# A 32-byte constant at the bottom of SBUF: moving every left-hand tile by half of 64 bytes

## The chip, the cores and the metric

The kernel runs on one core of one Trainium2 chip. The metric is the device time of one execution in microseconds (us); the time before is the median of 3 runs. The profile is that of one execution, with its own time beside it.

## What is computed

Band attention with 32 global tokens per sequence, followed by two MLPs of the same size, all in float32.

```python
# attention: 4 sequences x 8 heads, 32 global + 512 local tokens, head size 64
s_g = scale * q_g @ k_all.T;  out_g = softmax(s_g) @ v_all         # global rows see everything
s_l = [q_l @ k_g.T, band(q_l @ k_l.T, 32)] * scale                 # local rows: globals and a band
x = concat([out_g, softmax(s_l) @ [v_g, v_l]])                     # 2176 tokens x 512
# first MLP: ELU; second MLP: a smooth ReLU
x = elu(x @ w_in) @ w_out                 # 512 -> 2048 -> 512
h = x @ w2_in
g = where(h >= 1, h, where(h <= -1, 0, (h + 1)**2 / 4))
out = g @ w2_out
```

## The kernel before

The time after attention is matrix multiplication. Every float32 operand is split into a high and a low part (`xh`/`xl` for tokens, `gh`/`gl` for activations, `wh`/`wl` for weights), and each product is three matmuls: low weights with high tokens, high with low, high with high.

**Products.** `Up.products` (lines 258 and 261) multiplies tokens with w_in, `down` (line 342) and `down_rows` (line 359) multiply activations with w_out. In lines 261 and 342 the weights (128 columns) are the stationary operand, and 512 columns of `xh`/`xl` or `gh`/`gl` are the moving one. The 128 global tokens (index `GR`, tiles `xh4`, `xl4`) are handled the other way round in lines 258 and 359: a token or activation tile is stationary, and the weights move past it, 128 columns for each block of the hidden layer in line 258, 512 at once in line 359.

**Stages.** The 16 blocks of 128 hidden units of each layer are taken in ten chunks, `CHUNKS = [(3, 4, 3, 4, 2), (4, 3, 4, 3, 2)]`. The weights of a chunk lie in one of two rings, taken in turn: chunks 0, 2, 4, 6, 8 use ring 0 (`wh0`, `wl0`, three blocks deep), chunks 1, 3, 5, 7, 9 use ring 1 (`wh1`, `wl1`, four deep).

```python
n = max(len(fs) for _, fs in chunks[i::2])
ring[i] = [pool.tile([P, n, WCOLS], F32R, name=f"w{nm}{i}") for nm in "hl"]
```

While one ring is multiplied, `prep` fills the other: DMA of the raw float64 words, then ScalarE and VectorE. The `up` products of one chunk overlap the last `down` products of the one before (`LAG`), so there are short stretches in which both rings are used. In the profiled execution ring 1 is alone in use at about 192 to 264, 355 to 431, 498 to 574, 664 to 746 and 835 to 875 us, and ring 0 at 284 to 339, 593 to 647 and 765 to 819 us. Chunk 0 runs inside the attention.

**Where the numbers of matmuls come from.** A chunk of n blocks has 4 sequences x n blocks x 12 matmuls in line 261 and as many in line 342, and for the global tokens 12 in line 258 (n x 128 columns wide) and 3n in line 359 (512 wide).

**Between the products.** ScalarE and VectorE apply the curve and split the activations. A finished bank goes through `collect`: ScalarE copies it into one of two `ev` tiles (line 317), which a DMA writes or, on GpSimd's queue, adds to DRAM (lines 319 and 321). The last chunk of a layer loads these sums (`sum`, line 340), adds them (line 323), and splits them (lines 326 and 327) or writes the output (line 329).

**Order.** In the attention every instruction stays in program order (`Pinned`); behind it a planner orders them.

**Places in SBUF.** Pools take their room from the bottom in the order of opening, or from the top with `side="right"`. A tile begins at a multiple of 32 bytes, so a [128, 1] tile of 4 bytes takes 32. Places below are bytes from the start of a partition, and what is left of them modulo 64:

| tiles | side | place | modulo 64 |
|---|---|---|---|
| `mask_sb`, `eye_sb`, `half_sb` | left | 16512, 18048, 18560 | 0 |
| `one_sb`, the last constant | left | 18592 | 32 |
| `xh0` to `xl4` | left | 18624 to 88256 | 0 |
| `g`, `gh`, `gl` | left | 88256 to 112832 | 0 |
| ring 0: `wh0`, `wl0` | left | 112832, 125120 | 0 |
| `ev`, `acc_rows` | left | 137408 to 143552 | 0 |
| ring 1: `wh1`, `wl1` | right | 163808, 180192 | 32 |
| `wraw`, `top`, `power`, `rest`, `sum` (behind the attention) | right | 196576 and up | 32 |

All offsets inside these tiles that a matmul uses are multiples of 512 bytes, so an operand's place modulo 64 is that of its tile.

Of the kernel before, what the change touches and what calls it, by code (L numbers as in the profile page):

```python
# [9 lines left out]
F32 = mybir.dt.float32  # L10
# [15 lines left out]
P = 128  # L26
# [42 lines left out]
def band_attention_then_two_mlps(  # L69
# [20 lines left out]
    const = ctx.enter_context(tc.tile_pool(name="const", bufs=1))  # L90
# [7 lines left out]
    eye_sb = const.tile([P, P], F32, name="eye_sb")  # L98
    half_sb = const.tile([P, 1], F32, name="half_sb")
    one_sb = const.tile([P, 1], F32, name="one_sb")  # L100
    sizes = [SL] * B + [B * SG]
    xh = [xpool.tile([P, KT, n], F32R, name=f"xh{j}") for j, n in enumerate(sizes)]
    xl = [xpool.tile([P, KT, n], F32R, name=f"xl{j}") for j, n in enumerate(sizes)]
# [25 lines left out]
    eng = pinned  # L129
# [269 lines left out]
    with ExitStack() as actx:  # L399
# [46 lines left out]
        def spread_keys(b, hp):  # L446

            k_sb = loaded[b, hp][1]
            right = k_sb[:, KPAD:].rearrange("p (a c) -> p a c", a=NSUB)
            after = k_sb[:, SG + 32:KPAD].rearrange("p (a c) -> p a c", a=NSUB)  # L450
            glob = k_sb[:, 0:SG].rearrange("p (o c) -> p o c", o=1)

            if b + hp == 0:
                eng.vector.tensor_copy(right[:, :, 0:32], after)
                eng.scalar.activation(
                    right[:, :, 32:64], glob.to_broadcast([P, NSUB, SG]), AF.Copy
                )
                return
            eng.gpsimd.tensor_scalar(right[:, :, 0:32], after, 1.0, 1.0, ALU.mult, ALU.mult)
            eng.gpsimd.tensor_scalar(  # L460
                right[:, :, 32:64], glob.to_broadcast([P, NSUB, SG]), 1.0, 1.0, ALU.mult, ALU.mult
            )
# [239 lines left out]
        for c in range(2):  # L702
            for h in range(2):
                eng.vector.memset(head_sb[64 * c + 32 * h:64 * c + 32 * h + 32, h], 1.0)
        eng.vector.memset(one_sb, 1.0)
        spread_keys(*pairs[0])


# [102 lines left out]
        eng = free  # L811
# [132 lines left out]
```

## Time and profile before

| | |
|---|---|
| median of 3 runs | 880.3 us (880.19 to 883.67) |
| profiled execution, its own time | 882.43 us |
| its span, first to last instruction | 880.7 us |
| TensorE busy | 857.7 us (97%) |
| VectorE / ScalarE / GpSimd busy | 483.8 / 525.1 / 114.7 us |
| mean granted clock of TensorE | 0.994 |

In all views times are microseconds unless marked ns. PE is TensorE's matmul, PEld its weight load, DVE VectorE, ACT ScalarE, POOL GpSimd, SP SyncE; L342 is line 342 of the kernel. Matmuls overlap in the records, so the length of one (395 ns) is not what it costs; the cost is the distance from one start to the next. An operand list such as dn<-gh,wl gives the output, the moving operand and the stationary one, in this order. The helper of the pinned part gives all its instructions one line, L121.

### The profile page before, as it was taken

Reading aid. Unit: us, or ns where it says so; the run is one execution under the profiler, and the core shown is the slowest. Engines: PE = TensorE matmul, PEld = TensorE weight load, DVE = VectorE, ACT = ScalarE, POOL = GpSimd, SP = SyncE. Lnnn points to the kernel's source line nnn. Section 1 sums busy time; section 2 is a strip of 40 time slices with the busy share of each in tenths; the row PEclk is TensorE's granted clock in tenths of the full one; section 3 lists DMA queues with packets and bytes.
Section 4 is the critical chain, followed back from the end, with each engine's and each line's share of the span. In section 5 each row is a group of like instructions: output and inputs, shape, how many; then the busy total and the mean of one; then the engine's idle time right before and its main releaser. Section 6 shows DMA issues by size and latency. Waiting matters only on the chain.

```text
span 880.7 us, 15389 instructions
## 1 busy us (share of the span) xinstructions
PE 857.7 (97%) x6154; PEld 693.2 (79%) x6154; DVE 483.8 (55%) x971; ACT 525.1 (60%) x920; POOL 114.7 (13%) x178
## 2 busy tenths in 40 slices
PE   8899899999999999999999999999999899999997
PEld 5677778888888878888888888888888688888886
DVE  5898858867336743622279973277337422523244
ACT  5788766665436555544456776477665554665552
POOL 2222200001101121111110000001111111121200
PEclk9999999999999999999999999999999999999999
DMA  8988723534614773654354232025636431364476
GB/s 268 324 278 262 222 76 126 179 109 122 111 20 84 166 120 48 143 96 72 49 136 150 73 135 106 17 91 155 120 48 140 100 48 25 49 106 86 51 178 191
DMA packets 47544, 107.43 MB, mean 122 GB/s; under 512 B 7153, under 2 KB 7409, under 8 KB 43761
## 3 DMA queue, kind: packets, MB, share of 16 engines
q1 hardware_dynamic: 33360, 81.02, 27.7%
q0 software_dynamic: 13824, 25.17, 21.7%
q8 instruction: 48, 0.79, 0.4%
q10 hardware_dynamic: 288, 0.26, 0.1%
q14 instruction: 24, 0.19, 0.1%
HBM read 68.42 MB, written 38.01 MB: 121 GB/s over the span
## 4 chain that ended last, share of the span: by engine, by line
PE 50%; issue 36%; DMA 6%; POOL 3%; ACT 3%; DVE 1%; SPq 1%; POOLq 0%; DVEq 0%; ACTq 0%
PE dn L342 20%; PE up L261 20%; POOL sum L321 3%; DMA sum<-ev 2%; PE dn L359 1%; PE s L121 1%; DMA k_sb<-in_kT 1%; PE up L121 1%; DMA v_sb<-in_vwin 1%; PE pt L121 1%; PE po L121 1%; PE up L258 1%; ACT sn L121 1%; ACT pT L121 1%; SPq L121 1%
## 5 line engine op out<-in xcount | busy, mean ns | idle before, releaser
L342 PE MATMUL dn<-gh,wl 128*128 128x512 f32 x506 | 199.1, 395 | 4.7 <-ACT ev L317 4.7
L342 PE MATMUL dn<-gh,wh 128*128 128x512 f32 x506 | 199.7, 395 | 0.0
L342 PE MATMUL dn<-gl,wh 128*128 128x512 f32 x506 | 198.6, 395 | 0.0
L261 PE MATMUL up<-xh,wl 128*128 128x512 f32 x492 | 194.6, 396 | 0.0
L261 PE MATMUL up<-xh,wh 128*128 128x512 f32 x492 | 193.7, 394 | 0.0
L261 PE MATMUL up<-xl,wh 128*128 128x512 f32 x492 | 193.5, 393 | 0.0
L321 POOL DMA_DIRECT2D sum<-ev x96 | 85.1, 898 | 647.8 <-ACT ev L317 638.1
L281 DVE TENSOR_TENSOR g<-up,g 128x512 f32<-128x512 f32 (+1 forms) x69 | 47.1, 682 | 154.7 <-ACT g L274 154.7
L292 ACT ACTIVATE gh<-g 128x512 fp32r<-128x512 f32 x123 | 77.5, 631 | 76.5 <-DVE g L281 39.4
L317 ACT ACTIVATE ev<-dn 128x512 f32<-128x512 f32 x126 | 74.9, 595 | 74.7 <-DMA sum<-ev 65.6
L342 PEld LDWEIGHTS dn<-gh,wl 128*128 128x128 f32 x506 | 95.4, 189 | 27.9 <-ACT ev L317 6.8
L296 DVE TENSOR_TENSOR gl<-g,gh 128x512 fp32r<-128x512 f32 x123 | 84.7, 690 | 53.5 <-ACT gh L292 48.7
L342 PEld LDWEIGHTS dn<-gl,wh 128*128 128x128 f32 x506 | 95.5, 189 | 21.7
L342 PEld LDWEIGHTS dn<-gh,wh 128*128 128x128 f32 x506 | 95.6, 189 | 21.4
L261 PEld LDWEIGHTS up<-xh,wh 128*128 128x128 f32 x492 | 92.5, 188 | 21.0
L261 PEld LDWEIGHTS up<-xl,wh 128*128 128x128 f32 x492 | 92.5, 188 | 20.7
L261 PEld LDWEIGHTS up<-xh,wl 128*128 128x128 f32 x492 | 92.5, 188 | 20.3
L279 DVE SCALAR_TENSOR_TENSOR g<-up,g 128x512 f32<-128x512 f32 x64 | 43.3, 680 | 105.7 <-ACT g L269 105.7
L272 ACT ACTIVATE g<-up,half_sb 128x512 f32<-128x512 f32 (+1 forms) x69 | 46.6, 675 | 55.2 <-PE up L261 53.4
L267 ACT ACTIVATE g<-up 128x512 f32<-128x512 f32 x64 | 37.4, 586 | 56.4 <-PE up L261 56.2
L273 ACT ACTIVATE g<-g,one_sb 128x512 f32<-128x512 f32 (+1 forms) x69 | 49.3, 714 | 1.2
L191 ACT ACTIVATE top<-wraw 128x1024 f32<-128x1024 f32 x29 | 33.5, 1155 | 25.4 <-DMA wraw<-in_w 25.3
(115 smaller groups left out, 972.6 us busy)
## 6 DMA issues: line engine op xcount, KB each, us to landing
wraw<-in_w SPq DMA_DIRECT2D x29, 1024.0 KB, 5.3
sum<-ev POOLq DMA_DIRECT2D x96, 256.0 KB, 4.4
v_sb<-in_vwin SPq DMA_DIRECT2D x64, 260.0 KB, 4.7
sum<-ev SPq DMA_DIRECT2D x32, 256.0 KB, 2.0
sum<-sum SPq DMA_DIRECT2D x32, 256.0 KB, 3.2
k_sb<-in_kT SPq DMA_DIRECT2D x16, 288.0 KB, 4.4
q_sb<-in_qT SPq DMA_DIRECT2D x16, 272.0 KB, 4.3
outT<-sum SPq DMA_DIRECT2D x16, 256.0 KB, 3.1
```

The source lines that it names most:

```text
L121: return lambda *args, **kw: tc.keep_in_program_order(fn(*args, **kw))
L261: eng.tensor.matmul(self.ps, w, x, start=k == 0, stop=k == 3 * KT - 1)
L267: eng.scalar.activation(self.g, self.ps, AF.Exp)
L272: eng.scalar.activation(self.g, self.ps, AF.Relu, bias=half_sb, scale=-0.5)
L273: eng.scalar.activation(self.g, self.g, AF.Relu, bias=one_sb, scale=-1.0)
L279: eng.vector.scalar_tensor_tensor(g, self.ps, 0.0, g, ALU.max, ALU.subtract)
L281: eng.vector.tensor_tensor(g, self.ps, g, ALU.max)
L292: eng.scalar.activation(self.gh, self.g, AF.Copy)
L296: eng.vector.tensor_tensor(self.gl, self.g, self.gh.bitcast(F32), ALU.subtract)
L317: eng.scalar.activation(out, ps, AF.Copy)
L321: eng.gpsimd.dma_start(sums[layer, j, d], out, accum_op=ALU.add)
L342: eng.tensor.matmul(banks[d], w[:, d * P:(d + 1) * P], g, start=f == fs[0] and k == 0, stop=f == fs[-1] and k == 2,)
```

## The change

One more [128, 1] tile is allocated behind `one_sb`, and set to zero once by VectorE in the attention's opening. Nothing reads it.

```diff
     one_sb = const.tile([P, 1], F32, name="one_sb")
+    line_sb = const.tile([P, 1], F32, name="line_sb")
     sizes = [SL] * B + [B * SG]
...
         eng.vector.memset(one_sb, 1.0)
+        eng.vector.memset(line_sb, 0.0)
         spread_keys(*pairs[0])
```

Every left-hand tile that is allocated after the constants begins 32 bytes higher, and so lies at 32 modulo 64: tokens, activations, ring 0, `ev`, `acc_rows`. The right-hand tiles, ring 1 among them, stay where they were, at 32 modulo 64. `mask_sb` and `eye_sb` stay at 0.

## Rows read from the trace of the kernel before

**Rows 1.** The page's sections 1 and 2: busy us, share, instructions; granted clock.
```profile
PE 857.7 (97%) x6154; PEld 693.2 (79%) x6154; DVE 483.8 (55%) x971; ACT 525.1 (60%) x920; POOL 114.7 (13%) x178
PEclk9999999999999999999999999999999999999999
```

**Rows 2.** The page's section 5, costliest groups: count, busy us, mean ns, idle.
```profile
L342 PE MATMUL dn<-gh,wl 128*128 128x512 f32 x506 | 199.1, 395 | 4.7 <-ACT ev L317 4.7
L261 PE MATMUL up<-xh,wl 128*128 128x512 f32 x492 | 194.6, 396 | 0.0
```

**Rows 3.** Chain in order of time (start us, us, what, count), ring 1.
```profile
375.20 2.80 PE dn L342 x12
...
382.89 1.62 PE up L258 x7
...
400.81 5.60 PE up L261 x24
...
408.51 2.80 PE dn L359 x12
411.31 2.79 PE up L261 x12
...
852.00 2.10 PE up L261 x9
854.10 2.80 PE dn L342 x12
```

**Rows 4.** The same chain: ring 0 alone, and 754 to 763 with both.
```profile
312.43 2.77 PE up L261 x12
315.20 2.72 PE dn L342 x12
317.92 5.44 PE up L261 x24
...
754.48 2.73 PE up L261 x12
757.21 2.79 PE dn L342 x12
760.00 2.73 PE up L261 x12
...
805.45 2.04 PE dn L359 x9
```

**Rows 5.** Busy time by windows: PE, PEld, DVE, ACT, POOL, clock, DMA.
```profile
355.00:431.00 76.00, 76.00 (x330) 61.35 (x329) 26.19 (x37) 34.11 (x55) 12.37 (x14) 1.00 0.49 94
593.00:647.00 54.00, 54.00 (x244) 45.02 (x242) 28.56 (x39) 35.90 (x59) 8.01 (x9) 1.00 0.51 117
```

**Rows 6.** Timeline of 256-wide matmuls: ring 0 (453), ring 1 (840).
```profile
453.56 0.28 PE L258 MATMUL up<-wl,xh 128*128 128x256 f32 x1
...
454.16 0.40 PE L342 MATMUL dn<-gh,wl 128*128 128x512 f32 x1
...
840.07 0.28 PE L258 MATMUL up<-wl,xh 128*128 128x256 f32 x1
...
840.89 0.28 PE L258 MATMUL up<-wh,xl 128*128 128x256 f32 x1
```

**Rows 7.** Groups of VectorE and ScalarE by form: count, busy us, mean ns, idle.
```profile
L296 DVE TENSOR_TENSOR gl<-g,gh 128x512 fp32r<-128x512 f32 x123 | 84.7, 690 | 53.5 <-ACT gh L292 48.7 <-PE dn L342 3.5 <-PE up L261 0.7
L323 DVE TENSOR_TENSOR sum<-dn,sum 128x512 f32<-128x512 f32 x32 | 21.4, 687 | 8.3 <-PE dn L342 5.0 <-DMA sum<-sum 2.1 <-DMA outT<-sum 1.1
L292 ACT ACTIVATE gh<-g 128x512 fp32r<-128x512 f32 x123 | 77.5, 631 | 76.5 <-DVE g L281 39.4 <-DVE g L279 37.0
L326 ACT ACTIVATE xh<-sum 128x512 fp32r<-128x512 f32 x16 | 9.7, 625 | 3.8 <-DVE sum L323 3.8
```

**Rows 8.** The page's section 6: DMA issues, count, KB, median us to landing.
```profile
sum<-ev SPq DMA_DIRECT2D x32, 256.0 KB, 2.0
```

**Rows 9.** The tile view of outT, its line on landing times.
```profile
DMA to landing us min/median/max: 2.0/3.0/3.8
```

**Rows 10.** Timeline of the opening, VectorE.
```profile
1.97 0.06 DVE L121 MEMSET one_sb<- 128x1 f32 x1
...
3.71 0.43 DVE L121 COPY k_sb<-k_sb 128x512 f32<-128x512 f32 x1 [1.68 <-DMA k_sb<-in_kT]
```

**Rows 11.** Waits of PE, then of ACT, behind 192 us: total, times, longest.
```profile
PE dn L342 <- ACT ev L317: 4.7, 4, 2.6
...
ACT ev L317 <- DMA sum<-ev: 63.8, 48, 3.4
```

**Rows 12.** The chain around its stall in chunk 7.
```profile
691.62 6.25 DMA sum<-ev
698.63 5.08 PE dn L342 x14
703.71 2.80 PE up L261 x12
```

**Rows 13.** The windows view over that stall (columns as in rows 5).
```profile
694.00:702.00 8.00, 5.08 (x16) 3.37 (x15) 0.70 (x2) 3.79 (x7) 1.72 (x2) 0.81 0.84 118
```

## The prediction

> **What bounds the kernel now.** I read the page first. TensorE is busy 97% of the span, the other engines 60% at most, and the granted clock is 0.9 or more in every slice [rows 1]. The costliest groups are the matmuls of lines 342 and 261, nearly 3,000 of them, and all that they wait for is 4.7 us for an eviction [rows 2]. So behind the attention the time is the number of matmuls times the distance from one start to the next. The groups hide this distance, because the records of neighbours overlap. The chain of waits in order of time shows it: a piece "x12" that follows its neighbour without a break is twelve distances.
>
> Read so, the chain shows two paces that go by the ring. In chunks of ring 1, 24 matmuls of line 261 take 5.60 us and 12 of line 342 take 2.80 us, 233.3 ns each [rows 3]. In chunks of ring 0 they take 5.44 and 2.72 us, 226.7 ns each [rows 4]. From 754 to 763 us both rings are in use within microseconds: up products of ring 0 take 2.73 us, the down products of ring 1 between them 2.79 us, and the next up products 2.73 us again [rows 4]. Pieces of both lines have both paces, so it isn't the line; and neighbours in time differ as much as distant ones, so the other engines and DMA are no explanation. Nor is the clock: it is 1.00, the upper level of 2.4 GHz, in a stretch of either ring [rows 5]. Nor is the number of blocks in the chunk: chunk 9 has two, and its pieces from 852 us are 233.3 ns as well [rows 3].
>
> What sets the rings apart besides is their place. Ring 0 lies at 0 modulo 64 like every tile that it meets; ring 1 lies at 32 and meets tokens and activations at 0. One case tells more: for the global tokens the weights are the moving operand. Ring 1 is slow there too, 2.80 us for 12 in line 359, against 2.04 us for 9 (226.7 ns) with ring 0 [rows 3, 4]. So (moving, stationary) = (0, 0) is fast, and (0, 32) and (32, 0) are slow by the same amount. The trace holds no matmul of these lines at (32, 32), and the change makes all of them that.
>
> **The change part by part.**
>
> *Ring 1: 1,830 matmuls of 512 columns go from mixed places to equal ones.* Chunks 1, 3, 5, 7 have 4 blocks: 4 x 4 x 12 x 2 = 384, and 12 + 12 for the global tokens, 408 each, 1,632 together. Chunk 9 has 2 blocks: 192 + 6 = 198. The pace before: the pieces 2.80, 5.60, 2.80, 2.79, 2.10 and 2.80 us of rows 3 hold 81 matmuls (line 258 left aside) in 18.89 us, 233.2 ns. The pace of ring 0: 2.77, 2.72, 5.44, 2.73, 2.73 and 2.04 us hold 81 in 18.43 us, 227.5 ns [rows 4]. If equal places are what makes ring 0 fast, each matmul gains 5.7 ns: 1,830 x 5.7 = 10.4 us. Bounds: the best pair of rows gives 6.7 ns, 12.3 us; the slowest piece of ring 0 (2.77 us, 230.8 ns) against 233.2 gives 2.4 ns, 4.4 us. I take 10.4, because only one piece of the six is far from 227.
>
> *Ring 0: 1,386 matmuls of 512 columns go from (0, 0) to (32, 32).* Chunks 0, 2, 6, 8: 288 + 9 each; chunk 4: 192 + 6. They stay equal. Below nothing: 226.7 ns is the best pace in the trace, and I see no reason for a better one. Above: 5.7 ns each, 7.9 us, if a place at 32 costs by itself. I take 0. The nearest row that speaks on the place itself is line 258 with ring 1, where the moving operand is four separate runs of 128 columns, each beginning at 32: 1.62 us for 7, 231.4 ns [rows 3]. Line 359 has one run of 512, and 233.3 ns. Four misplaced beginnings cost no more than one, so it isn't the beginnings that cost.
>
> *The 256-wide matmuls of the global tokens*, 12 in each of chunks 4 and 9: with ring 0 five distances take 0.60 us, 120 ns each; with ring 1 seven take 0.82 us, 117 ns [rows 6]. A place at 32 costs nothing here, which again speaks for the pair and against the place. If ring 1 goes to 120 ns, 12 x 3 ns = 0.04 us are lost.
>
> *ScalarE, VectorE and DMA on moved tiles.* The trace has both places. VectorE's 512 columns take 690 ns with all SBUF operands at 0 (line 296), 687 with `sum` at 32 (line 323); ScalarE takes 631 ns from `g` at 0, 625 from `sum` at 32 [rows 7]. A 256 KB write lands 2.0 us after its issue from `ev` at 0, and `outT` from `sum` at 32 in 2.0 us at best [rows 8, 9]. Cost 0; and with these engines busy 55 and 60% [rows 1], a few ns would be hidden behind TensorE.
>
> *The memset* costs as much as that of `one_sb`, 0.06 us, on VectorE ahead of the copy of the first keys, which waits 1.68 us for their DMA [rows 10]. It vanishes in that wait; without it the start would come 0.06 us later. The planner that orders the work behind the attention has no more than this to react to; another order would show in the chain, and I add nothing for it.
>
> *Where the gain could be lost.* A faster TensorE asks for `ev` earlier. ScalarE waits 48 times for the DMA that frees `ev`, 63.8 us in all, but only 4 of the stalls reach TensorE [rows 11]. A burst of four evictions spans 12 matmuls, 2.80 us, and becomes 0.07 us shorter; even if ten bursts reached TensorE by this, that is under 1 us. The worst stall is in chunk 7, behind a DMA sum of 6.25 us in the chain, and 14 matmuls take 5.08 us after it [rows 12], because the clock falls behind the idle stretch: 0.81 over 694 to 702 us, so the lower level of 1.2 GHz for part of it [rows 13]. Stall and slow clock together are worth some 5 us: it may recur, vanish, or have a double. That is as large as the spread of the runs, 3.5 us. I add 0.
>
> The sum: 882.4 - 10.4 + 0.04 = 872.1 us for the profiled execution. The median of the runs is 2.1 us under that execution, so I forecast 880.3 - 10.4 = 869.9 us.
>
> **The rivals.**
>
> *The place itself costs (slower).* An operand at 32 may cost its 5.7 ns whatever the other does; both slow cases of the trace have one. Then ring 1 stays, and ring 0 loses 1,386 x 5.7 = 7.9 us: 888.2 us. If both operands count, ring 0 loses 11.4 ns and ring 1 another 5.7: 15.8 + 10.4 = 26.2 us, 906.5 us. For it: no row shows (32, 32). Against it: four runs cost what one does, and 256 columns cost nothing. The point where it decides is a pace at (32, 32) of 229.4 ns: 1,830 gains of 3.8 ns less 1,386 losses of 1.9 ns leave 4.3 us, no more than can be told from nothing; at 230.7 ns gains and losses are equal, and above it the kernel is slower.
>
> *The place modulo 64 has nothing to do with it (no change).* Ring 1 is also deeper, and lies at the other end of SBUF; the pace may hang on which region a tile is in. Then nothing moves: 880.3 us, within the 3.5 us by which runs differ. For it: chunk 9 excludes the depth in use, not the region. Against it: nothing in the trace separates region and modulus.
> The Trainium skill, TensorE: Matmul & The Clock Gate, section "Step-by-step: what each phase is for", says that weights and moving operand come through two independent SBUF ports, so that loading the next weights takes nothing from the running matmul. The Trainium skill, SBUF — State Buffer, section "Specifications (TRN2)", gives lines of 16 bytes, of which 32 is a multiple. By both, places would not matter, and the sum would be 0 in place of 10.4. That the rings have two paces, this trace shows against the plain reading of the first; why they do, it does not show.
>
> *The gain is eaten by `ev`.* A second stall like that of chunk 7 gives 869.9 + 5 = 875 us, still faster; it is within my own range.
>
> **How the numbers follow.** Equal places are fast: 0.62, with an own range of 866 to 875.5 us (12.3 us and a vanished stall's part below, a second stall above). The place itself costs: 0.22 (0.15 for 888.2, 0.07 for 906.5). Modulus without effect: 0.16. Within 0.5% (4.4 us, about what a measurement of this kernel can tell from no change) is the last case and a sliver of the first that the stalls exchange with losses elsewhere: faster 0.61, same 0.17, slower 0.22. The range reaches over the middle case to the milder slow one, 866 to 890 us, and leaves out 906.5 and the tails.
>
> **What the profile will show.** Right: pieces x12 in the chain of 2.72 to 2.75 us in every chunk, no difference left between up and down products around 754 us, 1,830 distances shorter by 5 to 6.7 ns, VectorE, ScalarE and DMA as before, the span some 10 us shorter. Wrong: ring 0 at 2.80 us (place itself), or ring 1 still at 2.80 and ring 0 at 2.72 (region). If the paces come out equal and fast but the time doesn't, it must stand in idle time of line 342 behind `ev`.

## The result

| | before | changed |
|---|---|---|
| median | 880.25 us (877.52 to 883.67, 4 runs) | 868.32 us (867.83 to 871.59, 4 runs) |
| profiled execution, its own time | 882.43 us | 871.59 us |
| its span | 880.7 us | 869.8 us |

The recorded ratio of the two is 0.9893 with a 95% interval of 0.9857 to 0.9929: 9.4 us of 880.25, with an interval of 6.2 to 12.6. The two medians of four runs lie further apart, by 11.9 us; in the experiments below, with 11 to 19 runs each time, the median of before was 877.20 to 877.57 us. The forecast was 869.9 us.

The chain of waits in order of time of the changed kernel (start us, us, what, number of instructions). All lines have moved by one: 343 was 342, 262 was 261, 360 was 359.

```profile
373.67 2.72 PE dn L343 x12
...
381.15 1.59 PE up L259 x7
...
398.63 5.44 PE up L262 x24
...
406.11 2.72 PE dn L360 x12
408.83 2.72 PE up L262 x12
...
683.45 6.19 DMA sum<-ev
690.39 5.07 PE dn L343 x14
695.46 2.72 PE up L262 x12
...
744.91 2.72 PE up L262 x12
747.63 2.72 PE dn L343 x12
750.35 2.72 PE up L262 x12
...
830.08 1.07 PE up L259 x9
...
843.67 2.72 PE dn L343 x12
```

These are the pieces of [rows 3] and the mixed stretch of [rows 4]. Every 2.80 of those rows has become 2.72, the 5.60 a 5.44: 226.7 ns a matmul in both rings. From 745 to 753 us, where up products of ring 0 and down products of ring 1 take turns, the step between the two paces is gone. For the 256-wide matmuls of chunk 9, nine take 1.07 us, 119 ns, against 117 before [rows 6].

VectorE and ScalarE kept their pace, and the stall of [rows 12, 13] is still there. The page's section 5 (count, busy us, mean ns, idle), then the windows view (PE, PEld, DVE, ACT, POOL, clock, DMA) over chunk 7's stall, changed kernel:

```profile
L343 PE MATMUL dn<-gh,wl 128*128 128x512 f32 x506 | 197.3, 392 | 4.2 <-ACT ev L318 4.1
L318 ACT ACTIVATE ev<-dn 128x512 f32<-128x512 f32 x126 | 75.0, 596 | 74.0 <-DMA sum<-ev 68.9
L297 DVE TENSOR_TENSOR gl<-g,gh 128x512 fp32r<-128x512 f32 x123 | 84.7, 690 | 52.9 <-ACT gh L293 52.3
```
```profile
686.00:694.00 8.00, 5.07 (x15) 3.45 (x14) 0.94 (x2) 4.03 (x7) 1.73 (x2) 0.79 0.81 121
```

The split on VectorE takes 690 ns with its tiles at 32 modulo 64, as it did at 0. The stall behind `ev`, from 683.45 us in the chain above, comes 8 us earlier and is as long as it was, and the clock falls to 0.79 over it.

### The profile page after: what moved, and what is told of

Its sections match the earlier page's. It is cut to its first block, busy times and chain, and to the rows that moved or that the text cites. A ratio compares the mean times of both kernels' runs of the same rounds, so it can differ in the third digit from the quotient of the medians.

```text
span 869.8 us, 15390 instructions
## 1 busy us (share of the span) xinstructions
PE 845.2 (97%) x6154; PEld 691.9 (80%) x6154; DVE 483.0 (56%) x972; ACT 524.5 (60%) x920; POOL 114.7 (13%) x178
## 4 chain that ended last, share of the span: by engine, by line
PE 50%; issue 35%; ACT 4%; DMA 4%; POOL 3%; DVE 2%; SPq 1%; POOLq 0%; ACTq 0%; DVEq 0%
PE dn L343 20%; PE up L262 20%; POOL sum L322 3%; DMA sum<-ev 2%; PE s L122 2%; PE dn L360 1%; ACT sn L122 1%; ACT pT L122 1%; PE pt L122 1%; PE up L122 1%; PE up L259 1%; PE po L122 1%; DMA v_sb<-in_vwin 1%; PE pog L122 1%; PE tg L122 1%
## 5 line engine op out<-in xcount | busy, mean ns | idle before, releaser
L343 PE MATMUL dn<-gl,wh 128*128 128x512 f32 x506 | 196.4, 391 | 0.0
L262 PE MATMUL up<-xh,wl 128*128 128x512 f32 x492 | 192.5, 391 | 0.0
L262 PE MATMUL up<-xh,wh 128*128 128x512 f32 x492 | 191.6, 389 | 0.0
L262 PE MATMUL up<-xl,wh 128*128 128x512 f32 x492 | 191.5, 389 | 0.0
```

Source lines behind the costliest of these rows:

```text
L262: eng.tensor.matmul(self.ps, w, x, start=k == 0, stop=k == 3 * KT - 1)
L343: eng.tensor.matmul(banks[d], w[:, d * P:(d + 1) * P], g, start=f == fs[0] and k == 0, stop=f == fs[-1] and k == 2,)
```

## The experiments

The open questions after the result: is it the pair of places, or the region, or the place of one operand; and is 64 the right modulus? In the tables below, "distance" is the mean from one start of a 512-wide matmul with stationary weights to the next start on TensorE, worked out from all starts in the trace, those of 290 ns and more left out (ring and block follow from the order of the matmuls); "off" is the place of the weights less that of the moving tile, in bytes modulo 256.

**1. Three kernels that move whole tiles.**

```diff
# e1: the kernel before, ring 1 down by 32 bytes (a pad at the top of its pool)
+        if i == 1:
+            eng.vector.memset(pool.tile([P, 1], F32, name="pad"), 0.0)
# e2: the kernel before, ring 0 up by 32 bytes (a pad below it)
+        if i == 0:
+            eng.vector.memset(pool.tile([P, 1], F32, name="pad"), 0.0)
# e5: the changed kernel, a constant of 64 bytes
-    line_sb = const.tile([P, 1], F32, name="line_sb")
+    line_sb = const.tile([P, 16], F32, name="line_sb")
```

> The kernel before, with ring 1 moved down by 32 bytes instead of everything else up: all operands of the matmuls at 0 modulo 64. Pair theory (a moving and a stationary operand at different places modulo 64 cost about 6 ns a matmul): every 512-wide matmul at 227 ns, as in the changed kernel, ratio to before 0.987 to 0.991. Place theory (32 is the better place, and only tokens there make ring 1 fast): ring 1 stays at 233 ns, ratio 1.000. Region theory (the move of the left-hand tiles counts, whatever the modulus): ratio 1.000.

> The kernel before, with ring 0 (and ev, acc_rows behind it) moved up by 32 bytes and tokens and activations left at 0: both rings at 32, all else at 0. Pair theory: ring 0 goes to 233 ns too, 1,386 x 5.7 ns = 8 us more, ratio 1.008 to 1.010. Region theory (something of ring 1 alone is slow): ring 0 stays at 227 ns, ratio 1.000.

> The changed kernel with a constant of 64 bytes in place of 32: the memset and a move of all left-hand tiles remain, their place modulo 64 is that of before. Pair theory with modulus 64: ring 1 back at 233 ns, ratio to before 1.000. Region theory, or a larger modulus in which 64 bytes count as well: ring 1 at another pace than 233 ns, ratio under 0.995 or over 1.005.

| kernel | ratio to before (95%) | off, ring 0 / 1 | distance, ring 0 / 1 |
|---|---|---|---|
| e1 | 0.9885 (0.9855 to 0.9916) | 0 / 0 | 227.2 / 226.9 ns |
| e2 | 1.0059 (1.0035 to 1.0082) | 32 / 32 | 233.3 / 233.3 ns |
| e5 | 1.0007 (0.9986 to 1.0028) | 0 / 224 | 227.5 / 233.2 ns |

The chain of waits of e2 shows chunk 8, ring 0, which had 2.72 us for 12 and 2.04 for 9 before:

```profile
778.33 2.80 PE dn L344 x12
781.13 2.12 PE up L260 x12
...
785.34 2.10 PE up L263 x9
```

Ring 0 can be made as slow as ring 1, and ring 1 as fast as ring 0, where it lies. Neither region nor the place 32 decides. e1 gives the whole gain without moving a token. e5 keeps the memset and a move of every left-hand tile, and gains nothing. Equal places were fast at 192 (e1), 224 (the changed kernel) and 0 modulo 256 (ring 0 of e5), so no one place is the fast one. The ratio of e2 is under what was expected (1.008 to 1.010), though its paces are as expected. Its profile has 2.5 us of waits for `ev` on TensorE where that of before has 4.7 [rows 11]; but the profiled execution of before (882.43 us) is itself 5 us above the median of before in that round (877.57), so the two profiles don't settle what the rest is.

**2. Which of neighbouring matmuls pays.** In the kernel before, ring 1's `wh1` goes to 0 and `wl1` stays at 32, by a pad between the two.

```diff
-        ring[i] = [pool.tile([P, n, WCOLS], F32R, name=f"w{nm}{i}") for nm in "hl"]
+        ring[i] = []
+        for nm in "hl":
+            if i == 1 and nm == "l":
+                eng.vector.memset(pool.tile([P, 1], F32, name="pad"), 0.0)
+            ring[i].append(pool.tile([P, n, WCOLS], F32R, name=f"w{nm}{i}"))
```

> The kernel before, with wh1 at 0 and wl1 at 32 modulo 64, all else at 0. In a run of matmuls (wl, xh), (wh, xl), (wh, xh) only the first has unequal places. If a matmul pays for its own pair, only the distance that begins with wl1 is 233 ns, the other two 227. If the load of the next weights pays while the present tokens stream, only the distance that ends with wl1's start (from the third of one triple to the first of the next) is 233. If either neighbour pays, both of these are slow and only the second is 227. Region theory: all three stay at 233.

TensorE's timeline of e3 (start us, us, instruction):

```profile
402.48 0.39 PE L346 MATMUL dn<-gh,wl 128*128 128x512 f32 x1
402.70 0.40 PE L346 MATMUL dn<-gh,wh 128*128 128x512 f32 x1
402.94 0.40 PE L346 MATMUL dn<-gl,wh 128*128 128x512 f32 x1
403.18 0.39 PE L346 MATMUL dn<-gh,wl 128*128 128x512 f32 x1
```

The distance that begins with wl1 is 0.22 us, the two others 0.24. The medians of ring 1's triples are 228, 232 and 239 ns, together 699: the same as three at 233. None of the expected patterns is it. The longest distance is the one that ends with the misplaced weights, which the second reading named, but the one ahead of it pays as well, and the sum is as if all three were misplaced. So one misplaced weight tile of three costs the triple as much as three do, and a fixed price for each unequal pair does not explain it.

**3. How far off.** In three kernels the blocks of ring 1 are set further apart, so that one execution holds four places side by side. `k` is 4 (e4), 1 (e7) or 16 (e6) elements of 4 bytes, and the edit is to the changed kernel.

```diff
+        if i == 1:
+            ring[i] = []
+            for nm in "hl":
+                t = pool.tile([P, -(-n * (WCOLS + k) // 16) * 16], F32R, name=f"w{nm}{i}")
+                t = t[:, 0:n * (WCOLS + k)].rearrange("p (n c) -> p n c", n=n)
+                ring[i].append(t[:, :, 0:WCOLS])
+            return
```

> The changed kernel with the four blocks of ring 1 a further 16 bytes apart each, so that against tokens and activations they lie 0, 16, 32 and 48 bytes off modulo 64 (ring 0 stays equal). Pair theory with lines of 64 bytes: block 0 at 227 ns, block 2 at 233, and blocks 1 and 3 slow too (233, or between). If only halves of 64 bytes count (0 to 31 against 32 to 63): block 1 at 227 and block 3 at 233. If lines of 16 bytes counted alone: all at 227, which the kernel before speaks against.

> The changed kernel with the blocks of ring 1 a further 4 bytes (one element) apart each: 0, 4, 8 and 12 bytes off modulo 64. If any difference of place costs: blocks 1 to 3 slow, 229 ns or more. If only halves of 64 bytes or lines of 16 count: all at 227.

> The changed kernel with the blocks of ring 1 a further 64 bytes apart each: 0, 64, 128 and 192 bytes off. Pair theory with modulus 64: all four at 227 ns. A modulus of 128 or 256: blocks 1 and 3, or 1 to 3, slow.

e6 was the surprise. Its chain of waits in chunk 3: block 1 (64 bytes off, 10 up products), block 2 (128, down and up), block 3 (192, down):

```profile
416.27 2.33 PE up L269 x10
418.60 2.79 PE dn L350 x12
421.39 2.78 PE up L269 x12
424.18 2.76 PE dn L350 x12
```

All lie at 32 modulo 64 like every other operand, and all are slow: 232.9, 232.6 and 229.5 ns over the execution. 64 is not the modulus. In e4 and e7 the longer tiles had also put block 0 at 128 bytes off for `wh1` and 192 for `wl1`, so that no block had the place that the expectation gave it; all blocks are slow there (229.6 to 232.6 ns), which fits a modulus of 256 and tells nothing of 4 or 16 bytes. For the next round the tiles were rounded up to 64 elements, which puts block 0 at 0 modulo 256.

**4. 64 or 256.**

```diff
# e9: the changed kernel, ring 1 down by 192 bytes
+        if i == 1:
+            eng.vector.memset(pool.tile([P, 48], F32, name="pad"), 0.0)
# e10, e11, e12: as above with k = 64, 4, 1
-                t = pool.tile([P, -(-n * (WCOLS + k) // 16) * 16], F32R, name=f"w{nm}{i}")
+                t = pool.tile([P, -(-n * (WCOLS + k) // 64) * 64], F32R, name=f"w{nm}{i}")
```

> The changed kernel with ring 1 moved down by 192 bytes: all operands still at 32 modulo 64, but ring 1 now 64 bytes off tokens and activations modulo 256. If the modulus is 64: all at 227 ns, ratio to before 0.987 to 0.991. If it is 256, as the blocks 64 bytes apart suggest: ring 1 at 233 to 234 ns, the whole gain lost, ratio 0.997 to 1.003.

> The changed kernel with the four blocks of ring 1 a further 256 bytes apart each: 0, 256, 512 and 768 bytes off tokens and activations. Modulus 256: all four blocks at 227 ns, as in the changed kernel. A modulus of 512 or more: blocks 1 and 3, or 1 to 3, at 229 ns or more. If a stride between blocks that isn't a power of two costs by itself: all but block 0 slow.

> The blocks of ring 1 a further 16 bytes apart again, with block 0 of both tiles now at a multiple of 256 from tokens and activations: 0, 16, 32 and 48 bytes off. Pair theory with modulus 256: block 0 at 227 ns, block 2 at 233 (the distance of the kernel before), blocks 1 and 3 between 229 and 235.

> The blocks of ring 1 a further 4 bytes apart, block 0 at a multiple of 256 from tokens and activations: 0, 4, 8 and 12 bytes off. If the exact place counts: block 0 at 227 ns, blocks 1 to 3 at 229 or more. If differences under 16 or 32 bytes are free: all at 227.

e9: ratio 1.0012 (0.9986 to 1.0037), ring 1 at 233.3 ns. With everything equal modulo 64, the whole gain is lost. The chain of waits of e9, ring 0 and ring 1 in turn as in [rows 4]:

```profile
747.50 2.75 PE up L264 x12
750.25 2.80 PE dn L345 x12
753.05 2.75 PE up L264 x12
755.79 2.80 PE dn L345 x12
```

e10, one execution, 869.08 us: the blocks 0, 256, 512 and 768 bytes off take 227.0, 227.1, 226.7 and 226.7 ns. These three multiples of 256 are free, and setting the blocks apart costs nothing by itself. e11 in chunk 3: block 1 (16 bytes off, up), block 2 (32, down and up), block 3 (48, down):

```profile
414.54 2.27 PE up L269 x10
416.81 2.79 PE dn L350 x12
419.60 2.79 PE up L269 x12
422.40 2.80 PE dn L350 x12
```

e12, the same stretch, 4, 8, 8 and 12 bytes off:

```profile
414.61 2.33 PE up L269 x10
416.94 2.77 PE dn L350 x12
419.71 2.77 PE up L269 x12
422.47 2.76 PE dn L350 x12
```

Together, ring 1's distance by how far it is off, modulo 256 (for e6, e10, e11 and e12 each value is from one execution, with blocks of other offsets as neighbours):

| off | 0 | 4 | 8 | 12 | 16 | 32 | 48 | 64 | 128 | 192 | 224 |
|---|---|---|---|---|---|---|---|---|---|---|---|
| ns | 226.7 to 229.0 | 232.1 | 230.8 | 229.7 | 228.3 | 232.8, 233.2 | 233.2 | 232.9, 233.3 | 232.6 | 229.5 | 233.2 |
| kernel | changed, e10, e6, e11, e12 | e12 | e12 | e12 | e11 | e11, before | e11 | e6, e9 | e6 | e6 | e5 |

Block 0 of e6, e11 and e12 (228.5 to 229.0) has slow blocks beside it; with fast neighbours, in the changed kernel and e10, it is 227.0. e11 ended between its expectations: 16 bytes off are almost free (median 227), 48 are not.

**5. What is left to gain.** The stalls of the changed kernel stand behind `ev`.

```diff
-    ev_p = ctx.enter_context(tc.tile_pool(name="ev", bufs=2))
+    ev_p = ctx.enter_context(tc.tile_pool(name="ev", bufs=4))
```

> The changed kernel with four ev tiles in place of two. What stalls were left in the changed kernel stood behind the DMA that frees ev: 4.2 us of idle time in line 343 and some 2 us at the lower clock behind the one in chunk 7. If that is their cause: they vanish, ratio to before 0.980 to 0.985 (861.5 to 867 us). If the DMA itself is the limit, the stall moves or stays: ratio 0.987 to 0.991 as in the changed kernel.

863.05 us (859.59 to 865.3), ratio to the kernel before 0.9835 (0.9806 to 0.9865): 14.5 us of the 877.54 us median of before in that round. Groups of e8 (count, busy us, mean ns, idle), then its windows view over chunk 7 and its neighbours:

```profile
L343 PE MATMUL dn<-gh,wl 128*128 128x512 f32 x506 | 196.5, 390 | 0.8 <-DVE sum L324 0.8
...
L318 ACT ACTIVATE ev<-dn 128x512 f32<-128x512 f32 x126 | 69.7, 599 | 2.7 <-PE dn L343 1.7
```
```profile
640.00:760.00 120.00, 120.00 (x533) 99.38 (x532) 55.67 (x75) 76.24 (x118) 18.79 (x22) 1.00 0.43 78
```

ScalarE's idle time ahead of the eviction is 2.7 us where it was 74.0, TensorE waits no more for it, and the clock stays at 1.00 through chunk 7. This version beats the kernel before. It was not run beside the changed kernel: its six runs (859.59 to 865.3 us) all lie under that kernel's four (867.83 to 871.59), and the intervals of the two ratios to before just overlap.

## Why the prediction was right

**The step that carried it**, ring 1 from 233.2 ns to the pace of ring 0, came as forecast: (32, 32) is as fast as (0, 0). It was a little under-sized. Ring 1's distance went from 233.2 to 226.9 ns, and 1,830 x 6.3 ns = 11.5 us stand where the sum had 10.4. The 227.5 ns that I took for ring 0 held a piece of 2.77 us, the first of [rows 4]. It stands behind three transposes (line 287, now 288) and has nothing to do with places, for it is 2.77 us in the changed kernel as well:

```profile
311.41 0.33 PE up L288 x3
311.74 2.77 PE up L262 x12
```

Without it the other five pieces give 227.0 ns, and the sum 1,830 x 6.2 = 11.3 us. Ring 0 itself went from 227.7 to 227.3 ns: 1,386 x 0.4 = 0.6 us more, where the sum had 0. That stands where the rings meet: the 48 distances that lead from a ring 0 matmul to one of ring 1 were 234.5 ns and are 226.8, and the 46 that begin right behind a ring 1 matmul and stay in ring 0 were 230.6 and are 226.9.

**What went the other way** is the attention. The piece in which the first sum is written stands in the two chains, before and then changed:

```profile
130.25 2.02 DMA sum<-ev
131.57 2.03 DMA sum<-ev
```

So 1.3 us are lost ahead of all this. I put it down to the execution, without having tested it: the first matmul of ring 1 starts between 165.9 and 170.7 us in the 14 profiles of this study, and in e9 and e10, which have the same left-hand places as the changed kernel, at 165.9 and 169.2. The sum is then 11.5 + 0.6 - 1.3 = 10.8, against 882.43 - 871.59 = 10.84 us measured. That the two agree to a tenth is partly luck: the waits for `ev` on line 342, now 343, changed by 0.6 us as well (4.7 to 4.1).

**The forecast of the time** came within 1.6 us of the median, and part of that is luck too. It took 10.4 us off a median of 880.3 us from three runs, some 3 us above the 877.2 to 877.6 us of the later rounds; the gain by the ratio is 9.4 us.

**The terms put at nothing** hold: on VectorE and ScalarE the splits of the activations take 690 and 631 ns as before, the evictions 596 ns where they took 595, and `sum` (line 323, now 324) 683 where it took 687; the 256-wide matmuls of chunk 9 take 119 ns in place of 117; the stall of chunk 7 recurred with 14 matmuls in 5.07 us.

**The rivals.** That the place itself costs is excluded by the result: with all operands at 32, the pace is the best of the trace. That the region decides is excluded by e1 and e2. The Trainium skill, TensorE: Matmul & The Clock Gate, section "Step-by-step: what each phase is for", says that loading the next weights takes nothing from the running matmul, by two independent ports. The forecast read from it that places would not matter, and this reading is not borne out here: e9 changes the changed kernel only in where ring 1 lies (and by one memset of the pad), and ring 1 takes 233.3 ns in place of 226.9. Whether it is the loading of the weights that slows the matmul, no run shows. The forecast had the right pair and, with the change's own words, the wrong modulus. Nothing in the trace of before could show it: of its two cases one is 0 bytes off, equal by either modulus, and the other 32, unequal by either. That the shift of 32 bytes worked is luck of the sizes: ring 1 lies 145,184 bytes above `xh0` before and 145,152 after, which is 567 x 256. With another size of a tile between them the same constant could have given an equal place modulo 64 and no gain, as e9 did.

**Left open**: why 256, why a triple with one misplaced tile costs as much as three, and why 256- and 384-wide matmuls don't pay (256-wide of chunk 9: 117.8 to 118.9 ns in the kernels with equal places, 116.8 to 120.2 with unequal ones; 384-wide of ring 0: 175.7 ns equal in e9, 175.1 unequal in e2). Whether tokens and activations must lie equal to each other, or each to the weights alone, wasn't tried.

## What to carry to other kernels

Read the distance between starts of like matmuls, by the tile that they read, before looking for idle time: a TensorE that was busy 97% of the span hid 1.1% here. Where two buffers of one role have two paces, compare their places to the other operand, and try 256 bytes as the unit; equal modulo 64 is not enough. Then look at what waits are left: two more 2 KB tiles gave, by the two ratios to before (14.5 against 9.4 us), half as much again as the change.

## What was not expected of the hardware

- Weights and moving tile of a 512-wide fp32r matmul at the same place modulo 256 bytes: 226.7 to 227.1 ns from start to start (blocks of ring 1, changed kernel and e10); off by 32 to 128: 232.6 to 233.3 ns, at a granted clock of 1.00 in a stretch of either pace [rows 5].
- Off by 4, 8, 12, 16 bytes: 232.1, 230.8, 229.7, 228.3 ns (one execution each). The Trainium skill, SBUF — State Buffer, section "Specifications (TRN2)", gives SBUF lines of 16 bytes and a price for crossing them. That 16 is cheaper than 4 to 12 fits with it; that 32 and 64 cost 6 ns does not follow from it.
- Which distance is long depends on the neighbours: 228, 232, 239 ns in a triple of which only the first matmul's weights are misplaced.
